# Attention, routing, experts and a bilinear layer on one core: scatters, zero rows, splits and two seams rearranged

## The chip, the cores and the metric

One core of a Trainium2 chip runs the whole kernel as one program. The metric is device time in microseconds of that core, the median of the runs.

## The reference

Three stages follow each other; all inputs are float32.

```
attention:  4 batches x 8 heads, 512 local and 32 global tokens, head size 64
  global tokens see all 544 keys; local tokens see the 32 global keys
  and the local keys within 32 positions; softmax; values
  -> x, 2176 rows of 512 (4 batches x 544 tokens)
experts:    rows with x @ w_skip > 0 go to the one expert (of 8) with the
  largest x @ w_gate;  x += p * (relu(x @ w1[e]) @ w2[e]);  others pass
bilinear:   out = ((x @ w_a) * (x @ w_b)) @ w_out,  inner width 1536
```

## The kernel before, in words

Instructions are put on each engine in the order in which the program emits them (a schedule written by hand); what an engine waits for is found from the tiles that an instruction reads and writes. TensorE is PE, VectorE DVE, ScalarE ACT, GpSimd POOL, SyncE SP; "PEld" is PE's weight load.

**Attention (0 to about 137 us).** Work goes in 16 pairs of heads (`pair(p)`, four pairs for each batch). A pair computes scores for pair p+2 (L957), masks (DVE, L969), exponentials (ACT, L980; then POOL copies the global columns, `smg`, L982), transposes (L994, L1004), values (L1020, L1029) and the turn into token rows (L1053). Within a pair four points are called slots, `4 * p` to `4 * p + 3`. `ROUTES` names slots at which a batch's routing is finished, and `SCATTERS` the slots at which each of its four token tiles is scattered by POOL (an indirect DMA into `xs`, L1246), the table of rows by expert. `xs` is first filled with empty rows: 16 writes of 128 rows by SP (L921), spread over the pairs by `ZEROS`. SP's transfers in a pair (loads, stores, zero rows, from pair 10 on expert weights) hang on ticks of PE: `pend` is a list, and each tick releases the next one.

At the end (`last_pairs`) SP loads the first rows of the two largest experts (`row<-xs`, L157), which waits for all scatters so far; PE turns them (L204) and the experts' first steps run between the last pair's pieces.

**Experts (about 137 to 285 us).** `WORK` lists ten pieces of an expert's rows; each has four steps of 256 hidden columns, 40 in all. Weights come as 512 KB pieces by SP (L152). float32 products are made from two parts of reduced length, so each piece is split: `hi` by ACT (L171) and `lo = raw - hi` by DVE (L181), two of the `lo` by POOL. A step is layer 1 (12 matmuls, L235 or L243), a copy `hr` by ACT, two transposes (`turn_h`, L1496), the copies `hh` (ACT) and `hl` (DVE, L1498), and layer 2 for the step before (6 matmuls, L1510). `HIS` and `LOS` say which early splits stand in which step. `positions()` works out the order of the experts in twelve small DVE operations, of which `some(3)` emits three at a time.

**The seam to the late stage (274 to 286 us).** Token rows of the first four tiles are loaded (`load_first`, L1532) and turned on PE into `xT` (L1554), onto which the last expert tile's output is added by a product with a selection matrix (L1580). `last` builds that output, scaled by its gate weight, in two parts `yh` and `yl`.

**Late stage (286 to 702 us).** `Late` runs the bilinear layer with a Strassen-like product (L527) in 24 steps; each also does the second product for the step before (`second`, L547), whose results are added into `out`. In the last round the sum so far is loaded, DVE adds (L553) and SP stores (L554).

Of the kernel before, what the change touches and what calls it, by code (L numbers as in the profile page):

```python
# [8 lines left out]
F32 = mybir.dt.float32  # L9
# [4 lines left out]
AF = mybir.ActivationFunctionType  # L14
ALU = mybir.AluOpType
# [16 lines left out]

ROUTES = (18, 34, 50)

SCATTERS = ((19, 23, 27, 31), (35, 39, 43, 47), (51, 51, 53, 55))

REUSE = 2

LEAD = 38

ZEROS = {0: (0, 4), 1: (4, 10), 2: (10, 14), 3: (14, 16)}

WORK = [(0, 0, 1), (1, 0, 1), (1, 1, 1), (3, 0, 1), (2, 0, 2), (0, 1, 1), (4, 0, 1), (5, 0, 1), (6, 0, 1), (7, 0, 1)]

# [44 lines left out]
class State:  # L89
# [83 lines left out]
        if 2 in ks:  # L173
            self.raws.pop(i)

    def split_lo(self, i, ks=(1, 2), pool=False):

        nc = self.tc.nc
        for k in ks:
            rv, hi, lo = self.parts_of[i].pop(k)  # L180
            (nc.gpsimd if pool else nc.vector).tensor_tensor(lo, rv, hi.bitcast(F32), ALU.subtract)  # L181
            a = 4 // k
            self.ws.setdefault(i, []).extend(z.rearrange("p (a f) -> p a f", a=a) for z in (hi, lo))

    def split(self, i, k, pool=False):
        if i < len(self.wsteps):
            self.split_hi(i, (k,))
            self.split_lo(i, (k,), pool)

    def turn_rows(self, k, psum):  # L190
        for f in self.turn_rows_hi(k, psum):
# [59 lines left out]
class Late:  # L251
# [286 lines left out]
    def second(self, b, g):  # L538

        nc = self.nc  # L540
        for q, t in enumerate(self.TILES[b]):
            acc = self.acc()
            for j in range(2):
                gh, gl = (x[:, 128 * q:128 * q + 128] for x in self.g[2 * j:2 * j + 2])
                wh, wl = self.wo[j]
                for z, (a, w) in enumerate(((gh, wh), (gh, wl), (gl, wh))):
                    nc.tensor.matmul(acc, lhsT=a, rhs=w, start=(j == 0 and z == 0), stop=(j == 1 and z == 2))  # L547
            n, dst = self.nout, self.out[128 * t:128 * t + 128, :]
            self.nout += 1
            if g == self.NM // 2 - 1:  # L550
                self.fetch_sums(n + 4)
                o = self.sums_in.pop(n)
                nc.vector.tensor_tensor(o, acc, o, ALU.add)  # L553
                nc.sync.dma_start(dst, o)  # L554
            else:
                o = self.o[n % len(self.o)]
                nc.scalar.activation(o, acc, AF.Copy)  # L557
                i = nc.gpsimd.dma_start(dst, o, accum_op=ALU.add if g else ALU.bypass)  # L558
                if g:
                    after(self.tc, i, [self.written[t]])  # L560
                self.written[t] = i.ins.name
                if n + 1 == self.tile_of[0][0]:
                    self.fetch_sums(n + 4)
            yield q
# [841 lines left out]
def experts(tc, const, dram, ident, w1, w2, x2d, xs, st, late):  # L1406
    nc = tc.nc
    with ExitStack() as es:
# [79 lines left out]
        def turn_h(i):  # L1488
            hh, hl, hr = hts.get(i, (None, None, None))
            if hr is None:  # L1490
                return
            hh, hl = st.parts(128)
            hts[i] = (hh, hl, None)
            pt = ps_h.tile([128, 2, 128], F32, tag="ph", name="pt")
            for j in range(2):
                nc.tensor.transpose(pt[:, j, :], hr[:, 128 * j:128 * j + 128], ident)  # L1496
            st.hh = nc.scalar.activation(hh, pt, AF.Copy).ins
            st.hl = st.hls[i] = nc.vector.tensor_tensor(hl, pt, hh.bitcast(F32), ALU.subtract).ins  # L1498

        def layer2(i):  # L1500
            k, q = steps[i]
            hh, hl, hr = hts.pop(i)
            h1, l1, h2, l2 = ws[i - NQ * (k >= REUSE)]
            if q == 0:
                accs[k] = [ps_o.tile([128, DM], F32, tag="acc", name="acc") for t in range(tiles(k))]
            for t, acc in enumerate(accs[k]):
                c = slice(128 * t, 128 * t + 128)
                terms = [(a, w, j) for a, w in ((hh, h2), (hh, l2), (hl, h2)) for j in range(2)]
                for z, (a, w, j) in enumerate(terms):
                    nc.tensor.matmul(acc, lhsT=a[:, j, c], rhs=w[:, j, :], start=(q == 0 and z == 0), stop=(q == NQ - 1 and z == 5))  # L1510
            if q == NQ - 1 and k < len(WORK) - 1:
                for t, acc in enumerate(accs.pop(k)):
                    xr = xts[k][2][t]
                    o = late.tmp[nstore[0] % 2][:, 0:DM]
                    nstore[0] += 1
                    nc.vector.scalar_tensor_tensor(o, acc, xr[:, 512:513], xr[:, 0:512], ALU.mult, ALU.add)
                    store(o, xr)
# [28 lines left out]

        xT = []

        def turn_first(rows, d0):
            for d in range(d0, d0 + 2):  # L1550
                xT.append((ps_x if d < 2 else ps_o).tile([128, 512], F32, tag="tp" if d < 2 else "acc", name="xT"))
            for t in range(4):
                for d in range(d0, d0 + 2):
                    nc.tensor.matmul(xT[d][:, 128 * t:128 * t + 128], lhsT=rows[t][:, 128 * d:128 * d + 128], rhs=ident,  # L1554
                                     is_transpose=True, start=(t == 0), stop=False)

        def last(rows):

            xr = xts[len(WORK) - 1][2][0]
            acc, = accs.pop(len(WORK) - 1)  # L1560
            rows_es.close()
            st.wes.close()
            late.open_x()
            oh, yh, yl = (late.g[z][:, 0:DM] for z in range(3))
            halves = slice(0, 256), slice(256, 512)
            for c in halves:
                nc.vector.tensor_scalar(y[:, c], acc[:, c], xr[:, 512:513], None, ALU.mult)
                nc.scalar.activation(yh[:, c], y[:, c], AF.Copy)
            for c in halves:
                nc.vector.tensor_tensor(yl[:, c], y[:, c], yh.bitcast(F32)[:, c], ALU.subtract)  # L1570
            late.plain(0, "b", "l", "m")
            o = late.tmp[0][:, 0:DM]
            nc.vector.tensor_tensor(o, y, xr[:, 0:DM], ALU.add)
            store(o, xr)
            late.load_x(1)
            turn_first(rows, 2)
            for z, a in enumerate((yh, yl)):
                for d in range(4):
                    c = slice(128 * d, 128 * d + 128)
                    nc.tensor.matmul(xT[d], lhsT=a[:, c], rhs=oh, start=False, stop=(z == 1))  # L1580
            late.first_x(xT)
            late.plain(0, "a")
            late.plain(1, "h", "b", "l", "m", "a")
# [8 lines left out]
            return i if i >= 2 * NQ else None  # L1592

        HIS = {2: ((4, 2), (5, 1)), 3: ((5, 2), (6, 1)), 4: ((6, 2), (7, 1)), 5: ((7, 2),)}
        LOS = {2: ((4, 1), (3, 2)), 3: ((4, 2), (5, 1), (6, 1)), 4: ((5, 2), (7, 1)), 5: ((6, 2),), 6: ((7, 2),)}

        for i in range(4, 7):
            st.fetch(i, (1,) if i < 6 else (0, 1))
# [3 lines left out]
        for i, (k, q) in enumerate(steps):  # L1602
            if i == NQ + 1:
                load_rows(3)
            if i > NQ:
                if q == 0 and k + 2 < len(WORK):
                    load_rows(k + 2)
                while st.nfetch <= min(i + AHEAD, len(st.wsteps) - 1):
                    st.fetch(st.nfetch)
            if i == FAR[-1] + 2:  # L1610
                far.close()
                late.open_first()
            if i == n - 7:
                late.take_raws()
            if i == n - 5:
                select()
            if i >= EARLY:
                layer1(i)
            if w1_of(i):
                st.split(w1_of(i), 1)  # L1620
            if q == (3 if k == 1 else 2) and k < len(WORK) - 1:
                turn_rows(k + 1)
                if k == 0:
                    st.split_hi(4, (1,))
            if i > 0:
                layer2(i - 1)
            if i < 3:
                st.split_lo(*((1, (2,)), (3, (1,)), (2, (2,)))[i])
            if i == 1:
                st.split_hi(3, (2,))  # L1630
            if i != 1:
                turn_h(i)
            if i == 0:
                turn_h(1)
            for j, z in HIS.get(i, ()):
                st.split_hi(j, (z,))
            for j, z in LOS.get(i, ()):
                st.split_lo(j, (z,), j > 5 and z == 1)
            if i in (3, 4, 6, 7):
                some(3)  # L1640
            if i > 2 * NQ:
                st.split(i - 1, 2)
            if i == n - 4:
                rows = load_first()
            if i == n - 1:
                late.plain(0, "h")
                turn_first(rows, 0)
            if n - NQ <= i < n:
                late.conv()
        layer2(n - 1)  # L1650
# [174 lines left out]
```

## Time and profile before

| | |
|---|---|
| median of 3 runs | 704.16 us (703.52 to 709.37) |
| the profiled execution | 704.23 us, its span 702.5 us |
| PE, DVE, ACT, POOL busy | 96%, 70%, 57%, 20% of the span |
| granted clock of PE, mean | 0.995 |
| moved by DMA | 154.86 MB, mean 220 GB/s |

Busy time of PE is near the span throughout, so what can be saved without less work lies where PE waits or runs at a lower clock.

### The profile page before, as it was taken

What the parts mean: (1) busy time and instruction counts of PE and PEld (TensorE: products, weight loads), DVE (VectorE), ACT (ScalarE), POOL (GpSimd) and SP (SyncE); (2) the same over time, 40 slices, a digit from 0 to 9 for tenths busy, and PEclk for the clock granted to TensorE, in tenths of its full rate; (3) what the DMA queues carried; (4) which work ended last, traced back from release to release, by engine and by line L of the source; (5) the groups of instructions that cost most, each with busy time, mean ns of one, the idle gap of its engine ahead of it and who ended that gap; (6) DMA issues with size and microseconds to landing.
All of it is one profiled execution on the core that took longest, in us unless ns stands there. A gap on an engine that the chain in (4) does not pass through costs nothing.

```text
span 702.5 us, 16719 instructions
## 1 busy us (share of the span) xinstructions
PE 677.2 (96%) x6323; PEld 605.8 (86%) x6323; DVE 493.4 (70%) x1276; ACT 397.6 (57%) x974; POOL 137.9 (20%) x215
## 2 busy tenths in 40 slices
PE   8989998799999999999999999999999999999996
PEld 5778877678898888779989999999999999999995
DVE  5677877698977998876985696856275656544444
ACT  5778777765857884566566644544354545443220
POOL 4002112162101120010011212322132222212000
PEclk9999999999999999999999999999999999999998
DMA  8897778599999946552686589995599669549853
GB/s 289 227 264 248 241 219 256 142 338 310 372 370 371 366 147 212 189 189 76 204 328 160 67 172 330 297 246 118 75 254 218 129 129 340 79 60 207 296 172 111
DMA packets 85997, 154.86 MB, mean 220 GB/s; under 512 B 8647, under 2 KB 40007, under 8 KB 84372
## 3 DMA queue, kind: packets, MB, share of 16 engines
q1 hardware_dynamic: 69092, 110.80, 48.2%
q0 software_dynamic: 15744, 42.87, 27.1%
q8 instruction: 52, 0.85, 0.5%
q14 instruction: 37, 0.30, 0.1%
q10 hardware_dynamic: 1072, 0.04, 0.1%
HBM read 105.95 MB, written 51.18 MB: 224 GB/s over the span
## 4 chain that ended last, share of the span: by engine, by line
PE 82%; DMA 5%; DVE 4%; ACT 4%; issue 3%; POOL 1%; SPq 1%; POOLq 0%; DVEq 0%; ACTq 0%
PE bank L527 32%; PE bank L547 19%; PE acc L1510 7%; PE ph L243 5%; PE bank L577 3%; DMA raw<-w 3%; PE o L1029 2%; PE sps L957 2%; PE o L1053 2%; PE ph L235 2%; PE tps L994 1%; ACT sm L980 1%; DMA xr<-xs 1%; PE o L1020 1%; PE bank L462 1%
## 5 line engine op out<-in xcount | busy, mean ns | idle before, releaser
L527 PE MATMUL bank<-xh,w 128*128 128x256 f32 (+1 forms) x1232 | 251.5, 290 | 0.1
L527 PEld LDWEIGHTS bank<-xh,w 128*128 128x128 f32 x1232 | 200.5, 189 | 4.2 <-DVE tmp L643 0.4
L527 PE MATMUL bank<-xl,w 128*128 128x256 f32 (+1 forms) x616 | 178.4, 290 | 0.0
L547 PE MATMUL bank<-woh,g 128*128 128x512 f32 x408 | 143.6, 395 | 1.1 <-ACT o L557 0.5
L527 PEld LDWEIGHTS bank<-xl,w 128*128 128x128 f32 x616 | 116.1, 188 | 4.2
L181 DVE TENSOR_TENSOR lo<-raw,hi 128x1024 fp32r<-128x1024 f32 x70 | 87.0, 1251 | 13.8 <-ACT hi L171 12.4
L547 PEld LDWEIGHTS bank<-woh,g 128*128 128x128 f32 x408 | 76.7, 188 | 15.7 <-ACT o L557 1.0
L547 PE MATMUL bank<-wol,g 128*128 128x512 f32 x204 | 80.1, 392 | 0.0
L171 ACT ACTIVATE hi<-raw 128x1024 fp32r<-128x1024 f32 x72 | 75.4, 1053 | 6.7 <-PE acc L1510 4.4
L601 ACT ACTIVATE g<-tmp 128x256 fp32r<-128x256 f32 (+1 forms) x88 | 37.8, 432 | 69.8 <-DVE tmp L643 68.9
L558 POOL DMA_DIRECT2D out<-raw x48 | 39.1, 815 | 141.7 <-ACT raw L557 121.9
L633 DVE TENSOR_TENSOR tmp<-bank,tmp 128x256 f32<-128x256 f32 (+1 forms) x44 | 18.8, 440 | 58.5 <-PE bank L527 58.4
L557 ACT ACTIVATE raw<-bank 128x512 f32<-128x512 f32 x48 | 28.5, 595 | 51.5 <-PE bank L547 51.5
L980 ACT ACTIVATE sm<-sm,nm 128x160 f32<-128x160 f32 x128 | 52.8, 419 | 7.8 <-DVE nm L969 7.8
L558 POOL DMA_DIRECT2D out<-o x37 | 29.6, 801 | 138.8 <-ACT o L557 100.8
L601 ACT ACTIVATE tmp<-bank 128x256 f32<-128x256 f32 (+1 forms) x88 | 34.5, 399 | 25.7 <-PE bank L527 21.8
L643 DVE TENSOR_TENSOR tmp<-bank,tmp 128x256 f32<-128x256 f32 (+1 forms) x88 | 38.9, 442 | 11.7 <-PE bank L527 10.2
L547 PEld LDWEIGHTS bank<-wol,g 128*128 128x128 f32 x204 | 38.3, 188 | 4.7
L639 DVE TENSOR_TENSOR g<-tmp,g 128x256 fp32r<-128x256 f32 (+1 forms) x88 | 38.3, 437 | 3.1 <-ACT g L601 1.4
L557 ACT ACTIVATE o<-bank 128x512 f32<-128x512 f32 x37 | 21.9, 595 | 32.0 <-PE bank L547 31.9
L243 PE MATMUL ph<-hi,xh 128*128 128x256 f32 x132 | 39.9, 302 | 0.0
L243 PE MATMUL ph<-lo,xh 128*128 128x256 f32 x132 | 37.3, 282 | 0.0
(266 smaller groups left out, 1290.6 us busy)
## 6 DMA issues: line engine op xcount, KB each, us to landing
raw<-w SPq DMA_DIRECT2D x64, 512.0 KB
out<-raw POOLq DMA_DIRECT2D x48, 256.0 KB, 4.4
out<-o POOLq DMA_DIRECT2D x37, 256.0 KB, 4.6
raw<-qk SPq DMA_DIRECT2D x28, 272.0 KB
xr<-x2d SPq DMA_DIRECT2D x25, 256.0 KB
raw<-wa SPq DMA_DIRECT2D x12, 512.0 KB
raw<-wb SPq DMA_DIRECT2D x12, 512.0 KB
raw<-wo SPq DMA_DIRECT2D x12, 512.0 KB
```

The costliest lines, as they stand in the source:

```text
L171: nc.scalar.activation(hi, rv, AF.Copy)
L181: (nc.gpsimd if pool else nc.vector).tensor_tensor(lo, rv, hi.bitcast(F32), ALU.subtract)
L243: nc.tensor.matmul(ph, lhsT=x[:, d, :], rhs=w[:, d, :], start=(z == 0), stop=(z == 11))
L527: self.nc.tensor.matmul(bank[:, 0:n], lhsT=w[:, k], rhs=x[:, xp, k], start=start and z == 0, stop=z == 5, skip_group_check=not start)
L547: nc.tensor.matmul(acc, lhsT=a, rhs=w, start=(j == 0 and z == 0), stop=(j == 1 and z == 2))
L557: nc.scalar.activation(o, acc, AF.Copy)
L558: i = nc.gpsimd.dma_start(dst, o, accum_op=ALU.add if g else ALU.bypass)
L601: cp = lambda o, i: nc.scalar.activation(o, i, AF.Copy)
L639: tt(g4[2 * j + 1][:, h], (u, p)[h][j], g4[2 * j].bitcast(F32)[:, h], ALU.subtract)
L643: tt(v, (b1, b2)[h][j][:, 0:n], v, ALU.mult)
L980: st_.exp = nc.scalar.activation(sm, sm, AF.Exp, bias=nm[:, hh, j:j + 1], scale=-1.0, accum_out=dens[p][:, k, j, hh:hh + 1]).ins
L1510: nc.tensor.matmul(acc, lhsT=a[:, j, c], rhs=w[:, j, :], start=(q == 0 and z == 0), stop=(q == NQ - 1 and z == 5))
```

## The change

- `SCATTERS`: batch 0's four tiles go at slots 24, 26, 28, 30 (before 19, 23, 27, 31), and batch 2's last tile at slot 53 (before 55).
- `ZEROS`: pairs 0, 1, 2, 3 and 5 take 3, 4, 3, 4 and 2 zero-row writes (before pairs 0 to 3 took 4, 6, 4, 2).
- All `lo` splits are on DVE; the two that POOL made are one step later, and in each step the first-layer split stands first. `some(3)` moves from steps 6 and 7 to 7 and 8.
- In the last expert step the turn of `hr` stands inside the layer 2 before, after its fourth matmul; `turn_first` goes by token tiles: tile 0 (four transposes) before the last layer 2, tiles 1 to 3 (twelve) after it.
- `last`: the plain split's `b` and `l` parts first; ACT makes `yh` from the accumulator with the gate weight as its scale, in one instruction of 512 columns; DVE makes `y` in one; the `m` part stands behind the store and the loads.
- The very last output tile is computed, added and stored in two halves of 256 columns, the second in another PSUM bank.

```diff
-SCATTERS = ((19, 23, 27, 31), (35, 39, 43, 47), (51, 51, 53, 55))
+SCATTERS = ((24, 26, 28, 30), (35, 39, 43, 47), (51, 51, 53, 53))
-ZEROS = {0: (0, 4), 1: (4, 10), 2: (10, 14), 3: (14, 16)}
+ZEROS = {0: (0, 3), 1: (3, 7), 2: (7, 10), 3: (10, 14), 5: (14, 16)}
...
-            (nc.gpsimd if pool else nc.vector).tensor_tensor(lo, rv, hi.bitcast(F32), ALU.subtract)
+            nc.vector.tensor_tensor(lo, rv, hi.bitcast(F32), ALU.subtract)
...
+            end = g == self.NM // 2 - 1 and len(self.sums_in) == 1 and not self.tile_of
+            halves = (slice(0, 256), slice(256, 512)) if end else (slice(0, 512),)
...
+            for c in halves:
+                if c.start:
+                    acc = self.bk[0][0]
+                for j in range(2):
...
+                        nc.tensor.matmul(acc[:, c], lhsT=a, rhs=w[:, c], start=(j == 0 and z == 0), stop=(j == 1 and z == 2))
+                if g == self.NM // 2 - 1:
+                    nc.vector.tensor_tensor(o[:, c], acc[:, c], o[:, c], ALU.add)
+                    nc.sync.dma_start(dst[:, c], o[:, c])
...
+                    if mid and z == 3:
+                        mid()
...
-        def turn_first(rows, d0):
+        def turn_first(rows, ts):
...
+            for t in ts:
+                for d in range(4):
...
-            for c in halves:
-                nc.vector.tensor_scalar(y[:, c], acc[:, c], xr[:, 512:513], None, ALU.mult)
-                nc.scalar.activation(yh[:, c], y[:, c], AF.Copy)
+            late.plain(0, "b", "l")
+            nc.scalar.activation(yh, acc, AF.Copy, scale=xr[:, 512:513])
+            nc.vector.tensor_scalar(y, acc, xr[:, 512:513], None, ALU.mult)
             for c in halves:
                 nc.vector.tensor_tensor(yl[:, c], y[:, c], yh.bitcast(F32)[:, c], ALU.subtract)
-            late.plain(0, "b", "l", "m")
...
             late.load_x(1)
-            turn_first(rows, 2)
+            late.plain(0, "m")
+            turn_first(rows, (1, 2, 3))
...
-        LOS = {2: ((4, 1), (3, 2)), 3: ((4, 2), (5, 1), (6, 1)), 4: ((5, 2), (7, 1)), 5: ((6, 2),), 6: ((7, 2),)}
+        LOS = {2: ((4, 1), (3, 2)), 3: ((5, 1), (4, 2)), 4: ((6, 1), (5, 2)), 5: ((7, 1), (6, 2)), 6: ((7, 2),)}
...
-                layer2(i - 1)
+                layer2(i - 1, (lambda: turn_h(i)) if i == n - 1 else None)
...
-            if i != 1:
+            if i not in (1, n - 1):
                 turn_h(i)
...
-                st.split_lo(j, (z,), j > 5 and z == 1)
-            if i in (3, 4, 6, 7):
+                st.split_lo(j, (z,))
+            if i in (3, 4, 7, 8):
                 some(3)
...
-                turn_first(rows, 0)
+                turn_first(rows, (0,))
```

## Rows read from the trace of the kernel before

**Rows 1.** Stages: length, busy us (instructions) by engine; clock, DMA share, GB/s.

```profile
20.00:60.00 40.00, 36.33 (x870) 31.61 (x872) 28.85 (x159) 28.68 (x113) 4.31 (x12) 1.00 0.99 278
...
160.00:270.00 110.00, 109.15 (x719) 97.32 (x718) 94.66 (x118) 81.92 (x128) 15.91 (x12) 1.00 0.93 317
...
286.00:690.00 404.00, 402.76 (x2617) 371.62 (x2616) 261.96 (x562) 196.15 (x449) 77.76 (x102) 1.00 0.72 188
```

**Rows 2.** Waits of PE: total us, times, longest.

```profile
PE eps L204 <- DMA row<-xs: 2.1, 1, 2.1
...
PE acc L1510 <- DVE hl L1498: 1.3, 1, 1.3
...
PE tp L204 <- DMA xr<-xs: 0.8, 1, 0.8
```

**Rows 3.** The chain that ended last, 116 to 138: start, us, what.

```profile
125.80 3.61 DMA xs<-xt,slu
...
129.68 2.55 DMA row<-xs
```

**Rows 4.** Timeline of POOL: start, us, instruction, [idle before, and its releaser].

```profile
118.86 0.99 POOL L1246 DMA_INDIRECT xs<-xt,slu  x1 [0.17 <-issue]
...
125.80 2.00 POOL L1246 DMA_INDIRECT xs<-xt,slu  x1 [0.17 <-issue]
```

**Rows 5.** Timeline of all engines, 128 to 146.

```profile
129.54 0.60 PE L1136 MATMUL ltp<-ident,xg 128*128 128x128 f32 x4
...
133.91 1.99 ACT L171 ACTIVATE hi<-raw 128x1024 fp32r<-128x1024 f32 x2
...
136.91 1.24 PE L1053 MATMUL o<-xi,ot 128*128 128x146 f32 x8
```

**Rows 6.** A stage of four us (columns as in rows 1).

```profile
132.00:136.00 4.00, 3.73 (x53) 3.01 (x53) 1.70 (x2) 2.49 (x3) 0.00 (x0) 0.57 0.81 245
```

**Rows 7.** Costliest groups: count, busy us, mean ns, idle before.

```profile
L557 ACT ACTIVATE o<-bank 128x512 f32<-128x512 f32 x37 | 21.9, 595 | 32.0 <-PE bank L547 31.9
```

**Rows 8.** The chain, 138 to 188.

```profile
146.12 10.79 DMA raw<-w
...
177.50 9.62 DMA xr<-xs
```

**Rows 9.** Timeline of DVE and POOL, 146 to 164.

```profile
152.72 3.01 POOL L181 TENSOR_TENSOR lo<-raw,hi 128x1024 fp32r<-128x1024 f32 x1 [1.70 <-ACT hi L171]
153.38 2.36 DVE L1422 SCALAR_TENSOR_TENSOR key<-run,leads 128x8 f32<-128x8 f32 x1
...
159.55 3.27 DVE L181 TENSOR_TENSOR lo<-raw,hi 128x1024 fp32r<-128x1024 f32 x1
...
163.08 1.21 DVE L181 TENSOR_TENSOR lo<-raw,hi 128x1024 fp32r<-128x1024 f32 x1
```

**Rows 10.** Timeline of PE at the seam, 276 to 285.

```profile
277.86 0.38 PE L1496 MATMUL pt<-ident,hr 128*128 128x128 f32 x2
...
279.93 0.44 PE L1554 MATMUL xT<-ident,xr 128*128 128x128 f32 x2 [0.41 <-DMA xr<-x2d]
280.12 0.72 PE L1510 MATMUL acc<-hi,hh 128*128 128x512 f32 x2
...
281.61 1.04 PE L1554 MATMUL xT<-ident,xr 128*128 128x128 f32 x8
282.80 2.10 PE L1580 MATMUL xT<-g,g 128*128 128x512 f32 x8 [0.15 <-ACT g L1568]
```

**Rows 11.** The end: DVE's last add, and a stage behind it.

```profile
695.64 0.69 DVE L553 TENSOR_TENSOR raw<-bank,raw 128x512 f32<-128x512 f32 x1 [0.68 <-PE bank L547]
...
697.00:699.00 2.00, 0.00 (x0) 0.00 (x0) 0.00 (x0) 0.00 (x0) 0.00 (x0) 0.95 0.44 153
```

**Rows 12.** Timeline of PE: first and last of its five long stalls, 20 to 60.

```profile
26.73 0.31 PE L1121 MATMUL gop<-vt,gpt 128*32 128x64 f32 x6 [1.01 <-issue]
...
50.04 0.33 PE L1029 MATMUL o<-pt,vt 128*64 128x64 f32 x2 [0.61 <-issue]
```

**Rows 13.** Timeline of POOL, 54 to 72.

```profile
64.47 0.29 POOL L982 COPY smg<-sm 128x128 f32<-128x128 f32 x1 [1.09 <-ACT sm L980]
```

More of the change, by code (lines that the diff above doesn't have):

```diff
@@ L174, in split_hi, with split_lo @@
             self.raws.pop(i)
-    def split_lo(self, i, ks=(1, 2), pool=False):
+    def split_lo(self, i, ks=(1, 2)):
         nc = self.tc.nc
@@ L180, in split_lo, with split @@
             rv, hi, lo = self.parts_of[i].pop(k)
-            (nc.gpsimd if pool else nc.vector).tensor_tensor(lo, rv, hi.bitcast(F32), ALU.subtract)
+            nc.vector.tensor_tensor(lo, rv, hi.bitcast(F32), ALU.subtract)
             a = 4 // k
             self.ws.setdefault(i, []).extend(z.rearrange("p (a f) -> p a f", a=a) for z in (hi, lo))
-    def split(self, i, k, pool=False):
+    def split(self, i, k):
         if i < len(self.wsteps):
             self.split_hi(i, (k,))
-            self.split_lo(i, (k,), pool)
+            self.split_lo(i, (k,))
     def turn_rows(self, k, psum):
@@ L542, in second @@
             acc = self.acc()
[L543 to L547, printed above, removed]
+            end = g == self.NM // 2 - 1 and len(self.sums_in) == 1 and not self.tile_of
+            halves = (slice(0, 256), slice(256, 512)) if end else (slice(0, 512),)
             n, dst = self.nout, self.out[128 * t:128 * t + 128, :]
@@ L552, in second @@
                 o = self.sums_in.pop(n)
-                nc.vector.tensor_tensor(o, acc, o, ALU.add)
-                nc.sync.dma_start(dst, o)
-            else:
+            for c in halves:
+                if c.start:
+                    acc = self.bk[0][0]
+                for j in range(2):
+                    gh, gl = (x[:, 128 * q:128 * q + 128] for x in self.g[2 * j:2 * j + 2])
+                    wh, wl = self.wo[j]
+                    for z, (a, w) in enumerate(((gh, wh), (gh, wl), (gl, wh))):
+                        nc.tensor.matmul(acc[:, c], lhsT=a, rhs=w[:, c], start=(j == 0 and z == 0), stop=(j == 1 and z == 2))
+                if g == self.NM // 2 - 1:
+                    nc.vector.tensor_tensor(o[:, c], acc[:, c], o[:, c], ALU.add)
+                    nc.sync.dma_start(dst[:, c], o[:, c])
+            if g < self.NM // 2 - 1:
                 o = self.o[n % len(self.o)]
@@ L1498, in turn_h, with layer2 @@
             st.hl = st.hls[i] = nc.vector.tensor_tensor(hl, pt, hh.bitcast(F32), ALU.subtract).ins
-        def layer2(i):
+        def layer2(i, mid=None):
             k, q = steps[i]
@@ L1547, in experts @@
         xT = []
-        def turn_first(rows, d0):
[L1550 to L1553, printed above, removed]
+        def turn_first(rows, ts):
+            if not xT:
+                xT.extend((ps_x if d < 2 else ps_o).tile([128, 512], F32, tag="tp" if d < 2 else "acc", name="xT") for d in range(4))
+            for t in ts:
+                for d in range(4):
                     nc.tensor.matmul(xT[d][:, 128 * t:128 * t + 128], lhsT=rows[t][:, 128 * d:128 * d + 128], rhs=ident,
```

## The prediction

> **What bounds the kernel now.** First the table of stages [rows 1]: TensorE (PE) is busy 36.33 of 40 us in the stretch 20 to 60, 109.15 of 110 in the experts (160 to 270) and 402.76 of 404 in the late stage. So PE is the bound nearly everywhere, and none of this change takes work from it: only the seams, where PE waits, can give anything back. Next the list of waits [rows 2]: the longest single wait of PE on a transfer is the 2.1 us on the first expert rows (row<-xs); then come 1.3 us on `hl` and 0.8 us on later rows (xr<-xs). The chain [rows 3] names the way into the first: a scatter into xs that lands 3.61 us after its start at 125.80, then the row load of 2.55 us. The profiled execution took 704.23 us for a span of 702.5; the median of the runs shown is 704.16, so a time saved in the span is taken off the median one for one.
>
> **Scatters of batch 2, (51, 51, 53, 55) to (51, 51, 53, 53).** Nothing is removed; the last scatter moves up by two slots. In GpSimd's (POOL's) queue the scatter before it starts at 118.86 and takes 0.99, the last one starts at 125.80 [rows 4], behind a copy of the pair in between. Moved, it starts at about 119.9 plus the gap of a queue, say 120.2, and lands 3.61 later, near 123.8. SyncE (SP) then loads the rows, 2.55 us: 126.4. PE is through with what stands before the rows' turning (four transposes from 129.54, 0.60) at 130.14 [rows 5], so the rows are there 3.7 us early and the wait of 2.1 goes. Behind this wait the profile shows a second loss: from 132 to 136 the granted clock is 0.57, a mean between its two levels 2.4 and 1.2 GHz, with PE busy 3.73 us [rows 6]. It fell right after the idle. If it doesn't fall, up to 3.73 x 0.43 = 1.6 us comes back as well. So this part is worth 2.1 at least, if the landing moves as said, and 3.7 at most. What is late next is ScalarE (ACT): it copies the turned rows (a 128x512 copy, 0.6, by the mean of [rows 7]), then makes two weight splits (1.99), then the copy for which the next transposes (L1053) wait (0.6). From 130.14: 0.6 for the turning, 0.6 + 1.99 + 0.6 on ACT give 133.9, against 136.91 in the trace [rows 5]. I take 2.9.
>
> Everything up to 157 must follow this shift. The weights that the chain meets next take 10.79 us from 146.12 [rows 8] because the queue is full, so they are early only if the fetches ahead of them are. These fetches are gated by the splits on VectorE (DVE) and by SP, which stood behind the same scatter; both move with it. The bounds are 0 (the transfers don't move) and the full 2.9; I take the full shift, since SP's own block ends over 5 us sooner.
>
> **Splits back on DVE.** Two GpSimd subtractions of 128x1024 go; two on DVE come, 1.21 each [rows 9], 2.4 in all. But the same rows show what GpSimd's cost DVE: while it worked from 152.72 for 3.01 us, DVE's `key` on 128x8 elements, started at 153.38, took 2.36 and ended with it; beside the second one a DVE split took 3.27 in place of 1.21. So DVE gets back some 2.2 + 2.1 and pays 2.4: 1.9 to the good. The 1.3 that PE waited for `hl` [rows 2] stood behind that `key`. I still count it at nothing: at the same moment ACT's copy of the next output stands behind a split whose weights land at 156.91 (146.12 + 10.79), so PE would wait there. Bounds: 0 to 1.3. What I count is further on. The chain into the rows at 187 is a load of 9.62 us from 177.50 [rows 8], long because of the weights queued ahead. The expert indices that SP needs before it may fetch on are four small DVE operations behind the blocked `key`; with them out about 2 us sooner, the queue is filled sooner, and the wait of 0.8 on xr<-xs should go. I take 0.8; bounds 0 and 2.1 (both waits). The splits' order (one step later each) keeps one step of lead over their use; if that lead were short, PE would wait a split's 1.21.
>
> **First rows by token tiles, and the order at the last step.** Between 277.86 and 282.80 PE [rows 10] does two transposes (0.38), eight of the rows' transposes in two halves, six matmuls (280.12 to 281.61, 1.49) and eight more transposes (1.04); then it multiplies by the selection at 282.80. Eight of these wait twice 0.41 for rows 2 and 3, ahead of six matmuls that don't need them, and the last waits 0.15 for ACT. After the change only token 0's four transposes stand there, and the twelve others, which need late rows, stand behind the matmuls. Moving the two transposes of `hr` into the previous layer 2 lets the `hh` copy and `hl` run behind two matmuls and the four transposes. Sum of the work: 0.38 + 2 x 1.04 + 1.49 = 3.95 of 4.94, so 1.0 comes back; counted start to start, without the pipeline's tail of each group (some 0.15 in four places), 1.5. I take 1.3. The ScalarE copy with the row's weight (about 0.6 on 512 columns) now runs off the accumulator at once, behind one plain split's half; both, at most 1.2, lie beside twelve transposes (12/8 of 1.04, 1.56). If that cover fell short, 0.4 would be lost. The moved scale, subtractions and store stay ahead of the next loads in each queue, and the store starts earlier.
>
> **Last tile in two parts.** Twelve matmuls of 256 columns replace six of 512: the same columns. The add took 0.69 from 695.64 and the transfer behind it is 0.44 of two us of all engines, 0.9 [rows 11]. In halves the last add is about 0.35 shorter and the transfer 0.4: 0.7. Bounds: -0.1 (twelve weight loads, one more issue on SP ahead of the last) and 1.0. The Trainium skill (SBUF — State Buffer, section "The DMA setup-cost knee") puts a fixed part of about 2 us, mostly completion, on every transfer and the rest by bytes at 436 GB/s; by that the half saved is an estimate of 0.3 us, which would make this part 0.6.
>
> **Zero rows and scatters of batch 0.** The same 16 writes go out over pairs 0 to 5, two of them in pair 5; four scatters start at slots 24 to 30 in place of 19 to 31. No wait of PE on these transfers shows. The stretch 20 to 60 has the DMA engines at a share of 0.99 [rows 1] and five stalls of PE put down to issue, from 1.01 (26.73) to 0.61 (50.04) [rows 12], some 3.7 in all. If these are instructions that arrive late through full engines, a thinner stream could give up to half back, 1.8; four scatters close together at slots 51 to 53 could add one such stall, 0.6. I take 0, since 14 of the 16 writes stay before 60. An added wait: the scatter at slot 24 waits for the last zero rows, and behind it on POOL stands the copy at 64.47 [rows 13], which PE's transposes of that pair need.
>
> **The sum.** 2.9 + 0.8 + 1.3 + 0.7 = 5.7 us: 704.2 - 5.7 = 698.5, faster by 0.8%. About 1% (7 us: 697.1 and 711.2) is what a measurement of this kernel tells from no change.
>
> **Rivals.** (a) The weights don't move. The queue is full up to 157, so they land at 156.91 whatever SP does, and PE waits there for what it gained: 2.9 falls away, 701.4. Against it: the engines are idle while SP stands behind the scatter. Chance 0.15. (b) The clock falls all the same. The rows show that it fell after a wait of 2.1 us, but PE had several half-idle us from 118 on too. Then the chain to L1053 runs at 1.2 GHz and 0.8 (2.9 - 2.1) is lost, or 1.6 if it falls in the expert steps: 699.3 to 700.1, 699.7 in the middle. The Trainium skill (TensorE: Matmul & The Clock Gate, "What's actually happening") says that throttled is the default state and activity releases it, and that the moment isn't tied to the kernel's start; by that rule the fall could stay. The trace agrees that idleness goes before it. Chance 0.12. (c) More comes back than I count: the `hl` wait (1.3) and half of the early stalls (1.8), 698.5 - 3.1 = 695.4. Chance 0.13. (d) Slower: the zero rows hold up POOL. If the last two, issued around 60, took as long as the long load of rows (9.62, [rows 8]), they would land at 69.6; with the scatter's 0.99 the copy behind it would come at 70.6 in place of 64.47, PE would stand 6.1 us and lose 1.6 to the clock as at 132: 698.5 + 7.7 = 706.2. It decides from a landing after 64 on. Against it: after 60 no load of that stage is late. Chance 0.05.
>
> **Range and chances.** My forecast has 0.55, with 696.8 to 699.8 as its own range. (a) and (b) reach up to 701.4, (c) down to 695.4; 695.0 to 701.8 leaves out (d) and the far ends. Faster by over 1%: all of (c) and a quarter of my own case, 0.27. Slower by over 1%: 0.03, from (d) at its worst. Within: 0.70.
>
> **What would show it.** Right: no wait of PE on row<-xs, a granted clock of 1.0 around 130 to 136, SP's row loads near 124; no DVE operation on 128x8 of over 2 us and no 3.27 split; the multiplication by the selection 4.2 us or more before 282.80 (5.0 with the 0.8); the last add 0.35 us long. Wrong: a wait of ACT or PE on raw<-w as long as the gain, a clock of about 0.5 elsewhere, POOL idle before the scatter at slot 24 on xs<-zrow, or PE stalls that grew between 116 and 122.

## The result, and the profile after

The changed kernel took 698.9 us (median of 14 runs, 694.8 to 703.7), the kernel before 704.6 on the same chip (14 runs): a ratio of 0.9912, 95% interval 0.9886 to 0.9938. The profiled execution took 698.71 us for a span of 696.9; the span before was 702.5, so 5.6 us are gone. Everything below asks where.

The table of stages, for the stretches of [rows 1]:

```profile
20.00:60.00 40.00, 35.60 (x853) 30.48 (x853) 27.84 (x156) 27.45 (x108) 3.06 (x11) 1.00 1.00 258
160.00:270.00 110.00, 110.00 (x727) 98.36 (x727) 94.41 (x122) 82.27 (x128) 15.23 (x11) 1.00 0.90 309
```

The profile now shows PE without idle time in the experts from 160 to 270 (110.00 of 110). But the list of its waits (total us, times, longest), from which the three of [rows 2] are gone, has a new first row, longer than any of them:

```profile
PE pt L1502 <- ACT hr L247: 3.5, 2, 3.3
```

Three rows of PE's timeline follow the shift (L1059 is the old L1053, L1502 the old L1496, L1516 the old L1510):

```profile
127.26 0.60 PE L1142 MATMUL ltp<-ident,xg 128*128 128x128 f32 x4
...
131.41 1.26 PE L1059 MATMUL o<-xi,ot 128*128 128x146 f32 x8 [0.18 <-ACT ot L1040]
...
154.01 0.44 PE L1502 MATMUL pt<-ident,hr 128*128 128x128 f32 x2 [3.26 <-ACT hr L247]
```

From `ltp` to L1059 it was 7.37 us [rows 5] and is 4.15: the wait for the first rows and the low clock behind it are gone, 3.2 us. The third row, a wait of 3.26, takes part of it back. Its chain (start, us, what):

```profile
140.91 11.69 DMA raw<-w
152.60 0.02 issue
152.63 0.03 ACT hi L171
152.65 0.94 issue
153.59 0.38 ACT hr L247
153.97 0.04 issue
154.01 0.44 PE pt L1502 x2
154.44 1.93 PE ph L243 x12
156.38 2.42 PE acc L1516 x6
```

The weights do land earlier, at 152.60 in place of 156.91 [rows 8]; counted from `ltp` that is 25.34 us in place of 27.37, so 2.03 of the 3.2 are left here. ACT's split of them (`hi`) stands in its queue ahead of the copy of `hr`, and PE waits for `hr`, which needs none of these weights (experiment 4). The price doesn't end there, as the stages from 152 on show (PE only: length, busy, clock, DMA share, GB/s):

```profile
152.00:154.00 2.00, 0.00 (x0) 1.00 0.53 135
154.00:156.00 2.00, 1.99 (x14) 0.77 0.84 249
156.00:158.00 2.00, 2.00 (x7) 0.50 1.04 266
158.00:160.00 2.00, 2.00 (x15) 0.87 0.94 338
```

After the idle the granted clock is at 0.50, the lower of its levels (1.2 GHz): 4.63 us from this `pt` to the next, where a run without the wait has 3.06 (151.38 to 154.44 in the kernel of the sixth experiment). So 1.57 more is lost; against the kernel before, with 3.10 at this place (158.32 to 161.42), it is 1.53.

DVE's small operation no longer stands behind POOL, and two splits together take 2.35 (DVE's timeline; compare [rows 9]):

```profile
145.62 2.35 DVE L181 TENSOR_TENSOR lo<-raw,hi 128x1024 fp32r<-128x1024 f32 x2
147.90 0.16 DVE L1428 SCALAR_TENSOR_TENSOR key<-run,leads 128x8 f32<-128x8 f32 x1
```

The seam, on PE's timeline (compare [rows 10]): only four transposes are left ahead of the last layer 2, no row waits, and from the first transposes to the multiplication by the selection it is 3.26 us, where it was 4.72 (278.08 to 282.80).

```profile
273.41 0.38 PE L1502 MATMUL pt<-ident,hr 128*128 128x128 f32 x2
...
274.10 0.60 PE L1562 MATMUL xT<-ident,xr 128*128 128x128 f32 x4
...
275.93 1.67 PE L1562 MATMUL xT<-ident,xr 128*128 128x128 f32 x12
277.36 2.11 PE L1588 MATMUL xT<-g,g 128*128 128x512 f32 x8
```

The end: the last add on DVE (compare [rows 11]), and the issues of the output on SP (count; least, median and longest ns; first and last start):

```profile
690.15 0.42 DVE L559 TENSOR_TENSOR raw<-bank,raw 128x256 f32<-128x256 f32 x1 [0.25 <-PE bank L557]
```

```profile
L560 SPq DMA_DIRECT2D out<-raw x13: 332/344/1567, 644.3 to 691.5; - x13
```

The add is 0.27 shorter. But from its end (690.57) to the end of the span it is 6.33 us, where it was 6.17: the issue of the first half takes 1.57 us on SP, and that of the second starts only at 691.5, 0.9 after its add. This delay isn't the whole reason, though: in the kernel of experiment 3 the last issue starts at 700.7, 0.1 after its add, and the way to the end is 6.27 all the same.

The 5.6 us, by points that both programs pass (PE's timeline):

| stretch | before | after | difference |
|---|---|---|---|
| start to `ltp` | 129.54 | 127.26 | -2.28 |
| `ltp` to the `pt` behind the late weights | 28.78 | 26.75 | -2.03 |
| on to the first transposes of xT | 119.76 | 120.09 | +0.33 |
| on to the multiplication by the selection | 4.72 | 3.26 | -1.46 |
| on to the end of the last add | 413.53 | 413.21 | -0.32 |
| on to the end of the span | 6.17 | 6.33 | +0.16 |

The +0.33 of the third row hides two things: the 1.53 lost to the clock, and 1.28 won at later rows (xr<-xs), for which PE waited before and doesn't now. From one `pt` to the next it took 5.21 there, and takes 3.93 (PE's timeline, before and after):

```profile
183.85 0.38 PE L1496 MATMUL pt<-ident,hr 128*128 128x128 f32 x2
186.46 1.36 PE L204 MATMUL tp<-ident,xr 128*128 128x128 f32 x8 [0.80 <-DMA xr<-xs]
189.06 0.38 PE L1496 MATMUL pt<-ident,hr 128*128 128x128 f32 x2
```

```profile
181.04 0.38 PE L1502 MATMUL pt<-ident,hr 128*128 128x128 f32 x2
...
184.97 0.38 PE L1502 MATMUL pt<-ident,hr 128*128 128x128 f32 x2
```

### The profile page after: what moved, and what is told of

Same layout as the page of the kernel before. It is cut to its first block, busy times and chain, and to the rows that moved or that the text cites. A ratio compares the mean times of both kernels' runs of the same rounds, so it can differ in the third digit from the quotient of the medians.

```text
span 696.9 us, 16731 instructions
## 1 busy us (share of the span) xinstructions
PE 674.1 (97%) x6329; PEld 604.6 (87%) x6329; DVE 490.6 (70%) x1278; ACT 397.0 (57%) x973; POOL 130.8 (19%) x213
## 4 chain that ended last, share of the span: by engine, by line
PE 80%; ACT 3%; DMA 3%; DVE 3%; issue 1%; POOL 0%; SPq 0%; DVEq 0%; POOLq 0%
PE bank L527 32%; PE bank L557 19%; PE acc L1516 8%; PE ph L243 6%; PE bank L583 3%; DMA raw<-w 3%; PE ph L235 2%; PE o L1059 1%; PE sps L963 1%; PE bank L462 1%; PE pt L1502 1%; ACT sm L986 1%; PE o L1035 1%; PE tps L1000 1%; PE tp L204 1%
## 5 line engine op out<-in xcount | busy, mean ns | idle before, releaser
L557 PE MATMUL bank<-woh,g 128*128 128x512 f32 (+1 forms) x412 | 143.7, 392 | 1.2 <-ACT o L563 0.5
L181 DVE TENSOR_TENSOR lo<-raw,hi 128x1024 fp32r<-128x1024 f32 x72 | 87.0, 1221 | 11.9 <-ACT hi L171 10.8
L557 PE MATMUL bank<-wol,g 128*128 128x512 f32 (+1 forms) x206 | 80.4, 390 | 0.0
L243 PE MATMUL ph<-hi,xl 128*128 128x256 f32 x132 | 37.5, 284 | 0.0
```

Source lines behind the costliest of these rows:

```text
L181: nc.vector.tensor_tensor(lo, rv, hi.bitcast(F32), ALU.subtract)
L243: nc.tensor.matmul(ph, lhsT=x[:, d, :], rhs=w[:, d, :], start=(z == 0), stop=(z == 11))
L557: nc.tensor.matmul(acc[:, c], lhsT=a, rhs=w[:, c], start=(j == 0 and z == 0), stop=(j == 1 and z == 2))
```

## The experiments

They ran in four groups, each on one chip, and the kernel before took 711.6, 706.3, 706.9 and 710.1 us there. Most of the difference between chips lies before `ltp`, by the profiles of the kernels with edits (`ltp` starts at 127 to 131 us in the second and third group but for one kernel with a new wait ahead of it, at 135 to 138 in the first and fourth). So each time is given as its ratio to the kernel before of its own group, and beside it stands the stretch from `ltp` to the first transposes of xT, which leaves that part out: 148.54 before, 146.84 after.

**1. The last scatter back at slot 55, in the changed kernel.**

```diff
-SCATTERS = ((24, 26, 28, 30), (35, 39, 43, 47), (51, 51, 53, 53))
+SCATTERS = ((24, 26, 28, 30), (35, 39, 43, 47), (51, 51, 53, 55))
```

> The changed kernel with only the last scatter of batch 2 back at slot 55. Theory (the scatter gates SP, and SP gates the weights): the rows wait of 2.1 us is back near 129, the row loads start near 129 instead of 123.7, the weights land near 156.9 instead of 152.6, and the end comes 2.8 later (the shift of the accumulation at 161.58 against 158.80 in the two profiles): 701.7. Rival (the weights land when the full queue lets them, whatever SP does): the rows wait is back, but the weights land at 152.6 all the same, PE's wait of 3.26 for hr shrinks by what it waits earlier, and the time stays within 0.7 of the changed kernel: 698.9 to 699.6.

Measured: 0.9981 (0.9953 to 1.0009), 709.15 us; stretch 147.51. PE's waits:

```profile
PE eps L204 <- DMA row<-xs: 2.4, 1, 2.4
PE pt L1502 <- ACT hr L247: 1.6, 2, 1.4
```

The wait on the rows is back, and the wait for `hr` has shrunk to 1.4. ACT's split that waits for the weights:

```profile
161.83 1.06 ACT L171 ACTIVATE hi<-raw 128x1024 fp32r<-128x1024 f32 x1 [1.47 <-DMA raw<-w]
```

It starts 27.0 us behind `ltp` (134.79), where it was 25.4 in the changed kernel (152.63) and 27.4 in the kernel before (156.93). So the weights do follow the scatter, by 1.7 here, as the theory had it. Yet the stretch is only 0.7 longer than the changed kernel's, as the rival had it for the time: behind this shorter wait the clock stays at 1.00 (160 to 168), and the 1.57 that the changed kernel lost isn't lost.

**2. The last scatter at 53, alone, in the kernel before.** The line above the other way round.

> The kernel before with only the last scatter of batch 2 at slot 53; nothing else of the change. Theory (the scatter is the largest part, and what it gains is partly taken back by the weights): ltp starts 2 us earlier with no wait on row<-xs, the copy of hi that waits for raw<-w holds up hr for 2 to 3.5 us near 153, and 2.5 to 3 us remain at the end: 701.6 to 702.1. Rival 1 (nothing is taken back, as the sum of the prediction had it): 2.9 to 3.4 remain and no wait of over 1 us near 155. Rival 2 (all is taken back): the accumulation after the weights is where it was at 161.6, and the end is within 0.7: 703.9 to 704.6.

Measured: 0.9975 (0.9947 to 1.0004), 709.7 us; stretch 147.73, 0.8 less than before. From `ltp` to L1053 it took 4.15 (138.24 to 142.39) in place of 7.37, so the rows' wait goes by this edit alone; what is left of its 3.2 at the transposes of xT is 0.8. The first theory said that most is taken back, and it is, but not at the weights: PE passes the `pt` behind them at 163.41, 25.17 behind `ltp`, where it was 28.78 before, so here the weights followed in full. Most is lost at later rows:

```profile
192.77 1.56 PE L204 MATMUL tp<-ident,xr 128*128 128x128 f32 x8 [1.61 <-DMA xr<-xs]
```

From the `pt` ahead of them (189.34) to the next (196.68) it took 7.34 in place of 5.21.

**3. Two splits back on POOL, in the old order.**

```diff
-LOS = {..., 3: ((5, 1), (4, 2)), 4: ((6, 1), (5, 2)), 5: ((7, 1), (6, 2)), ...}
+LOS = {..., 3: ((4, 2), (5, 1), (6, 1)), 4: ((5, 2), (7, 1)), 5: ((6, 2),), ...}
-                st.split_lo(j, (z,))
+                st.split_lo(j, (z,), j > 5 and z == 1)
```

> The changed kernel with the two subtractions back on POOL and the splits in their old order. Theory (POOL's subtraction holds DVE's small operations, and these hold SP's fetches): DVE's key on 128x8 takes over 2 us again, PE waits 0.7 to 0.9 on xr<-xs near 184 and the end is 0.8 to 1.3 later: 699.7 to 700.2. Rival (the wait at 187 went with the earlier weights, and not with the splits): key takes over 2 us but no wait on xr<-xs comes back, and the time is that of the changed kernel, 698.9 within 0.5.

Measured: 0.9943 (0.9919 to 0.9966), 707.09 us; stretch 146.06. POOL's and DVE's timeline, and PE's waits:

```profile
158.14 2.99 POOL L181 TENSOR_TENSOR lo<-raw,hi 128x1024 fp32r<-128x1024 f32 x1 [1.71 <-ACT hi L171]
158.80 2.35 DVE L1428 SCALAR_TENSOR_TENSOR key<-run,leads 128x8 f32<-128x8 f32 x1
```

```profile
PE tp L204 <- DMA xr<-xs: 1.4, 1, 1.4
PE acc L1516 <- DVE hl L1504: 1.3, 1, 1.3
```

`key` started in POOL's subtraction and ended with it again (161.15 and 161.13). The Trainium skill (SBUF — State Buffer, "SBUF: two separate sides") says that the two share one pair of ports as an exclusive lock when a DVE operation has two SBUF inputs; these rows agree. Behind it PE waits 1.3 for `hl` (PE's timeline):

```profile
162.72 0.72 PE L1516 MATMUL acc<-hi,hl 128*128 128x512 f32 x2 [1.26 <-DVE hl L1504]
163.72 0.44 PE L1502 MATMUL pt<-ident,hr 128*128 128x128 f32 x2 [0.28 <-ACT hr L247]
```

This wait comes with POOL's splits, but it costs nothing here: `hr`, whose copy stands behind the weights on ACT (163.30), comes later still. The 1.4 on xr<-xs looks like the theory, but the next kernel, of the same group, has the splits on DVE and waits 1.6 there, since its PE comes sooner. What the splits do change is when SP issues these rows: at 182.38 here and at 181.17 there, 44.2 and 43.2 us behind `ltp`. So the theory's chain to SP is there with some 1 us (one profile each), and the wait isn't the splits' doing alone.

**4. ACT's split one step later.**

```diff
-HIS = {..., 4: ((6, 2), (7, 1)), 5: ((7, 2),)}
+HIS = {..., 4: ((6, 2),), 5: ((7, 1), (7, 2))}
```

> The changed kernel with ACT's split of the weights of step 7 (first part) one step later, behind the copy of hr of step 5. Theory (the wait of 3.26 us at 154 is one of order on ACT's queue: hr stands behind a split whose weights land at 152.60, and PE doesn't need those weights yet): the wait goes, the granted clock stays 1.0 over 154 to 160 (1.5 us more), and 3.3 to 4.8 us come off: 694.1 to 695.6. Rival (the weights set the time themselves): PE waits as long one or two steps later, at the first use of those weights or of the next ones, near 157 to 165, and the time stays within 1 of 698.9.

Measured: 0.9913 (0.9886 to 0.9940), 704.79 us; stretch 144.27, 2.6 less than the changed kernel's 146.84. No wait for `hr` over 0.3, a clock of 1.0 from 150 to 270. That alone would prove little, as experiment 3 on the same chip, with the old order on ACT, had no longer wait for `hr` either (it stood behind the one for `hl`); but the copy itself moved, from 163.30 there, behind a split for whose weights ACT had stood 2.15, to 160.09 here, 25.1 and 22.1 us behind `ltp`. So PE didn't need those weights, and the theory of order holds; but 1.6 us are now waited on xr<-xs, so a part only. The same 0.9913 as the changed kernel's is no contradiction nor a proof: that one wasn't in this group.

**5. The changed kernel again, and three others.**

> The changed kernel once more, as it is, beside three others, since the chip of the first four experiments gave the kernel before 711.6 us in place of 704.6, and stalls of PE put down to issue between 20 and 128 us of 7.3 to 11.9 us in sum, against 6.1 (before) and 3.5 (after) in the two profiles. Expected, if the chip changes only these stalls: a ratio within 0.986 to 0.994 as measured first. If the gain hung on the first chip: a ratio above 0.994.

Measured: 0.9910 (0.9875 to 0.9946), 700.38 us; stretch 146.75, wait for `hr` 3.2. The first result repeats, with 8.1 us of stalls put down to issue in this profile where the first had 3.5; so such stalls change by several us from one run to the next.

The zero rows and the scatters of batch 0 as before:

```diff
-SCATTERS = ((24, 26, 28, 30), ...
+SCATTERS = ((19, 23, 27, 31), ...
-ZEROS = {0: (0, 3), 1: (3, 7), 2: (7, 10), 3: (10, 14), 5: (14, 16)}
+ZEROS = {0: (0, 4), 1: (4, 10), 2: (10, 14), 3: (14, 16)}
```

> The changed kernel with the zero rows and the scatters of batch 0 as they were in the kernel before. Prediction's step (worth nothing, bounds -1.8 to 0.6): the same time as the changed kernel within 0.7 us, stalls put down to issue between 20 and 60 as large. Rival (a burst of zero rows delays instructions): the stalls between 20 and 60 grow by 1 to 2 us and so does the time.

Measured: 0.9913 (0.9883 to 0.9943), 699.6 us. This part of the change is worth nothing that can be measured.

Then most zero rows later (`ZEROS = {3: (0, 4), 5: (4, 8), 6: (8, 12), 7: (12, 16)}`, scatters at 33, 34, 36, 37):

> The changed kernel with 12 of the 16 zero rows later, four each in pairs 5, 6 and 7 (after about 58 us, where the DMA share was 0.6), four in pair 3, and the scatters of batch 0 at slots 33 to 37. Theory (PE's stalls put down to issue are instructions that come late through full DMA engines): the stalls between 20 and 60, 3.5 to 8 us in the profiles so far, fall by half or more, and 2 to 4 us come off the changed kernel on the same chip. Rival (the loads of q and k fill the engines whatever the zero rows do, or the stalls are no matter of the DMA): the stalls stay, and the time is that of the changed kernel within 1 us. A second rival: late scatters hold up POOL's copies near 80 us and PE waits there, 1 to 2 us slower.

Measured: 0.9988 (0.9966 to 1.0010), 705.83 us. The stages, first of the changed kernel (second profile), then of this one:

```profile
20.00:40.00 20.00, 17.54 (x430) 15.44 (x430) 13.04 (x70) 14.35 (x59) 1.59 (x6) 1.00 0.95 238
40.00:60.00 20.00, 14.84 (x365) 12.70 (x357) 14.08 (x86) 12.61 (x50) 1.45 (x5) 1.00 1.01 251
60.00:80.00 20.00, 18.79 (x480) 16.73 (x484) 13.66 (x66) 14.44 (x55) 5.83 (x10) 1.00 0.68 213
```

```profile
20.00:40.00 20.00, 20.00 (x513) 17.92 (x514) 15.22 (x83) 16.06 (x64) 1.88 (x7) 1.00 0.54 165
40.00:60.00 20.00, 19.45 (x494) 16.57 (x494) 16.94 (x97) 15.70 (x62) 1.58 (x6) 1.00 0.94 286
60.00:80.00 20.00, 15.90 (x356) 13.91 (x352) 11.59 (x63) 11.09 (x45) 1.16 (x4) 0.91 0.92 247
```

And DVE's timeline of this kernel:

```profile
91.51 0.69 DVE L1073 TENSOR_TENSOR xt<-o,den 128x512 f32<-128x512 f32 x1 [8.32 <-DMA xs<-xt,slu]
```

With no zero rows before 38 us PE had no stall from 20 to 40. Nor had it one of over 0.3 in the 20 us behind, with eight zero-row writes and a DMA share of 0.94. They came back later (3.7 us at 70), and 7.5 us more at 92, which that row explains: the scatters were so late that DVE waited 8.3 us to write the batch's buffer again. So this kernel couldn't tell what the zero rows alone cost.

**6. Three edits on the order of queues.** Experiment 4's; the fetch of step 7 ahead of the four stores on SP; one half of the last output issued by ACT.

```diff
-        st.store_last()
         st.fetch(7)
+        st.store_last()
...
-                    nc.sync.dma_start(dst[:, c], o[:, c])
+                    (nc.sync if c.start else nc.scalar if end else nc.sync).dma_start(dst[:, c], o[:, c])
```

> The changed kernel with three edits: the split of the first part of step 7 one step later on ACT; the fetch of step 7's weights ahead of the four stores of the last batch on SP; the first half of the last tile's output issued by ACT in place of SP. Theory: where PE waits 3.3 us for hr near 154 in the changed kernel, it no longer does, with up to 1.5 us of clock behind it; the last issue on SP ends 0.6 after the last add in place of 1.4, so the end comes 0.8 sooner; 0.8 in all on a chip where that wait isn't there, 4 to 5 where it is. Rival (the weights only come as the queue lets them, and the stores' delay holds up the rows): PE waits 2 us or more for the weights or for xr<-xs somewhere between 155 and 190, and only the 0.8 of the end remains.

Measured: 0.9900 (0.9866 to 0.9934), 699.51 us, beside 700.38 for the changed kernel in the same group; stretch 144.23, 2.5 less. PE's first wait from 120 to 300:

```profile
PE tp L204 <- DMA xr<-xs: 1.9, 1, 1.9
```

Both theories have their part: the wait for `hr` is gone, with the clock's loss, and 1.9 us are waited for rows. The stretch is that of experiment 4 (144.27), so the fetch ahead of the stores adds nothing that shows. The medians are only 0.9 apart and their intervals overlap, so the 2.5 is shown by the profiles and not by the time. From the last add to the end it is 5.82 us where nine profiles with both halves issued by SP had 6.01 to 6.63, so about 0.5 at that place too.

**7. The expert rows two steps earlier in SP's order, on top of 6.**

```diff
-                if q == 0 and k + 2 < len(WORK):
-                    load_rows(k + 2)
+                if q == 2 and k + 3 < len(WORK):
+                    load_rows(k + 3)
```

> The three edits of the kernel before this one (split of step 7 later on ACT, step 7's fetch ahead of the stores, one half of the last output issued by ACT), and the expert rows loaded two steps earlier in SP's order, ahead of eight weight loads. Theory (PE's 1.9 us at xr<-xs near 180 is the order of SP's queue, not of the DMA's bytes): the wait goes, no wait of PE between 140 and 270 is over 0.5, and the stretch from ltp to the first transposes of xT takes 142.3 in place of 144.2: 1.9 us off, a ratio of 0.987 to 0.989. Rival (the engines are full, and something else is late instead): a wait of 1 to 2 us on weights or on hr appears between 155 and 200 and the stretch stays at 144 to 145.

Measured: 0.9840 (0.9811 to 0.9870), 695.07 us. The rows that PE waited for are issued at 165.62, where they stood at 171.40 behind more weight loads, and the wait is gone. PE's timeline:

```profile
128.57 0.60 PE L1142 MATMUL ltp<-ident,xg 128*128 128x128 f32 x4
...
270.87 0.60 PE L1562 MATMUL xT<-ident,xr 128*128 128x128 f32 x4
```

270.87 - 128.57 = 142.30 us, as the theory had it. This is the fastest kernel of the study: 6.2 us less than before in this stretch, where the change itself gave 1.7.

**8. The zero rows spread over pairs 2, 3, 5 and 6, four each, scatters at 29, 30, 31, 31.** First in the changed kernel:

> The changed kernel with the 16 zero rows in pairs 2, 3, 5 and 6, four each (none while the first loads of q and k fill the engines), and the scatters of batch 0 at slots 29 to 31, before the batch's buffer is written again near 83 us. Theory (PE's stalls put down to issue come from instructions that arrive late through full DMA engines, and the zero rows fill them): the stretch 20 to 40 is free of stalls, as it was with the late zero rows, the stalls in 20 to 80 add up to 2 us or less where the changed kernel had 3.5 and 8.1 in two profiles, and 2 to 3 us come off its 0.991 of the kernel before: 0.987 to 0.989. Rival (the same bytes cost the same stalls wherever they go, as the stall of 3.7 us at 70 with the zero rows of pairs 5 to 7 suggests): the stalls come in 40 to 80 instead, and the ratio stays at 0.990 to 0.993.

Measured: 0.9941 (0.9917 to 0.9966), 701.66 us. PE was busy 19.61 us of 20 to 40, but 16.89, 17.93 and 18.02 in the three stretches of 20 us after it; 6.8 us of stalls in all. The rival's stalls are there: fewer in 20 to 40, more behind it. The time is a little slower than the rival's range, too, though its interval reaches into it. Then together with the edits of 7:

> Both sets of edits in one kernel. If the two theories hold and are independent: stalls of 2 us or less in 20 to 80, the stretch from ltp to xT at 142.3, and 0.984 to 0.986 of the kernel before (5 us off the changed kernel's 0.991). If only one of the two holds: 0.987 to 0.989. If neither: 0.990.

Measured: 0.9888 (0.9848 to 0.9927), 698.47 us, 3.4 us more than without, with intervals that just overlap. In the profiles 2.0 of it lies before `ltp`, as if the moved zero rows cost here too, and 1.3 between `ltp` and xT (143.63 in place of 142.30).

**9. The old seam, in the changed kernel.** `turn_first`, `last` and the order of the last step as in the kernel before.

> The changed kernel with the first rows turned by halves of d again and the last step in its old order (hr's transposes behind layer 2, eight transposes and the wait for late rows ahead of the six matmuls). Prediction's step (1.3 us): from the first transposes of xT to the multiplication by the selection 4.7 us or more in place of the 3.1 to 3.3 of seven profiles with the new order, one or two waits on xr<-x2d of 0.4 back, and 1.3 to 1.6 us later at the end: a ratio of 0.993. Rival (what the seam gives is lost at the next wait, for the late stage's first loads): the seam is 4.7 long, but the end comes within 0.5 of the changed kernel: 0.991 to 0.992.

Measured: 0.9985 (0.9959 to 1.0011), 708.77 us. PE's timeline:

```profile
281.92 0.71 PE L1562 MATMUL xT<-ident,xr 128*128 128x128 f32 x4
283.02 0.44 PE L1562 MATMUL xT<-ident,xr 128*128 128x128 f32 x2 [0.39 <-DMA xr<-x2d]
284.12 0.44 PE L1562 MATMUL xT<-ident,xr 128*128 128x128 f32 x2 [0.67 <-DMA xr<-x2d]
...
286.99 1.19 PE L1588 MATMUL xT<-g,g 128*128 128x512 f32 x4 [0.15 <-ACT g L1576]
```

The seam is 5.07 us long, 1.1 of it waits for late rows; with the new order eleven profiles of this study have 3.06 to 3.55. So 1.5 to 2.0 belong to it. The ratio is 0.7% above the changed kernel's 0.9912, some 5 us, which is more than that; but the changed kernel wasn't measured on this chip, so the rest can't be put down to the seam.

## Why the prediction was right, and where only its sum was

The time (698.5 against 698.9) came out of terms that were wrong in both directions, so that it fits so closely is luck: from `ltp` to the transposes of xT 1.7 us came of 3.7 that were counted (scatter and splits), at the end 0.1 of 0.7, and 2.3 came before `ltp`, where nothing was counted.

- **Scatter, 2.9.** Its mechanism was right: rows loaded from 123.67, no wait, a clock of 1.0 from 126 to 150, 3.2 us by L1059. The step that failed is "I take the full shift". The weights did move, by 4.31, but 2.28 of that lies before `ltp`, so 2.03 of 3.2 were left at the `pt` behind them, and the clock took 1.57 of that: 0.5 stayed at this place. In experiment 2 the weights followed in full, and the gain was lost at the rows behind them. At the transposes of xT the scatter is worth 0.7 and 0.8 in experiments 1 and 2. I had looked for the limit at SP and the full queue (rival a) and at the clock (rival b). It was ACT's order that let PE stand for weights it didn't need (experiment 4), and the clock fell there, behind an idle of 3.3, and not at the place where I had it. So both rivals came true in part, further on, and two of my signs of being wrong were there: ACT stands 3.35 for raw<-w ahead of its split at 152.63, and the clock is at 0.50 from 156 to 158.
- **Splits, 0.8.** DVE's rows came as worked out, and the wait on xr<-xs went, with 1.28 in place of 0.8. But the reason given is only a part of it. From `ltp` to SP's issue of these rows it is 47.2 us before, 44.4 with the scatter alone (experiment 2), 44.2 with POOL's splits back in the changed kernel (3) and 43.3 in the changed kernel: some 2.8 are the scatter's and some 1.0 the splits'. And the wait is gone only as PE comes there later than in experiments 4 and 6, held up by `hr`: it was back at 1.6 and 1.9 where that was taken away, and experiment 7 puts it down to SP's order. The 1.3 on `hl` was rightly counted at nothing: before too, `hr` (157.90) came later still. What the splits alone are worth in time no run shows.
- **Seam, 1.3.** Right: 1.46 in the pair of profiles, with no wait left, and lost again with the old order.
- **Last tile, 0.7.** Mis-sized: the add is 0.27 shorter, the way from it to the end 0.16 longer, 0.1 in all; the kernel of experiment 2, with the tile whole, has a way of 5.51, so it may be a loss. The lower bound (-0.1, for one more issue on SP ahead of the last) was nearer than the 0.7. With one half on ACT the way is 5.82, 5.66 and 5.10 (experiments 6, 7 and the second kernel of 8), with the tile whole 6.17 and 5.51, so no gain over the whole tile is shown. The tile whole in the changed kernel wasn't tried.
- **Zero rows, 0.** Right (0.9913 with the old ones).
- **Not in the sum:** 2.3 us before `ltp`. In the profile before, four stalls between 118.17 and 120.37, 1.7 in sum, stand there; the stretch 100 to 120 has PE busy 17.75 us, and 19.05 or 19.06 in seven profiles of the changed kernel and its variants where the kernel before took 704.6 to 706.9 (19.28 in the eighth, with the late zero rows). Where it took 710 or more (experiments 1 to 4 and 9), such stalls are there with the change as well. No run tells which edit removes them, or whether it is an edit; it isn't the zero rows, since the kernel with the old ones has 19.06 too. Nor are the DMA engines full there; a stage of two us in the kernel before (columns as in rows 1):

```profile
118.00:120.00 2.00, 0.84 (x6) 0.54 (x6) 0.00 (x0) 0.60 (x3) 1.69 (x3) 1.00 0.27 75
```

So 2.3 of the 5.6 us have no cause that is shown.

## What to carry to other kernels

When a wait is removed, follow the next late transfer and ask what stands behind it in the in-order queue of the engine that consumes it: here 3.3 us of PE stood behind a split that nobody needed yet, and 1.9 behind a row load that was queued after eight weight loads, and each went with an edit of a line or two. A part of the program that shifts is worth only what the next meeting with an unshifted transfer leaves of it; sum up to that point, not to the end. In the stage where the DMA engines are full, the three kernels with the zero rows elsewhere had their stalls elsewhere and no better ratio than the kernels they were made from; and the last transfer in two halves gained nothing that shows.

## What the runs showed of the hardware

- The stalls of PE put down to issue reach 4.2 us (the kernel of experiment 4, at 53 us; the 7.5 in experiment 5 has its own reason), and their sum between 20 and 128 us ran from 3.5 to 11.9 in the profiles of one program family. With the DMA share at 0.54 there were none, but at 0.94 none of over 0.3 either (the kernel with the late zero rows in experiment 5, 20 to 40 and 40 to 60), and the four at 118 to 120 came at a share of 0.27. The Trainium skill (Runtime: NRT & Kernel Launch, "Instruction fetch mechanics") says that instructions come by a DMA queue in blocks of 16 KiB and that this cost is mostly hidden; the trace agrees on the blocks in one queue (52 packets, 0.85 MB, of kind instruction), while a second queue has 37 of half that size (0.30 MB). Whether a late one makes these stalls is open: a packet of the first queue begins within the stalls of 4.2 and 3.7 us, only one of the second within those of 1.72 (the changed kernel) and 2.27 (experiment 7), and neither within another of 1.72 (experiment 2, at 34 us).
- The same kernel before took from 704.6 to 711.6 us in median on five occasions, so 1% hangs on the chip. In the profiles of the kernels with edits `ltp` starts at 127 to 131 or at 135 to 138 us, so most of it lies before `ltp`.
- An output issue on SP took 0.34 us in the median; the longest, where two stand close together at the end, 0.87 to 1.65 in nine profiles. On ACT the same issue took 0.37.
